# Group order, scratch rows, attention and W3's tails in a fused attention and MLP kernel

## The chip, the cores and the metric

One core of a Trainium2 chip runs the whole kernel. The metric is the device time of one execution in microseconds.

## The reference

With x normalised per row (xn), the output is x + A(xn) + B(xn), for 2048 tokens of 576 channels, all in float32.

```python
def _A_ref(x, wqkv, wo):          # 32 heads of 18, window of 8 keys, every second token
    q, k, v = ...                 # x @ wqkv, split by heads
    idx = pos[:, None] - off[None, :]            # off = 0, 2, ... 14; masked below 0
    logits = einsum("bhsd,bhswd->bhsw", q, kg) * scale
    o = einsum("bhsw,bhswd->bhsd", softmax(logits), vg)
    return o @ wo
def _B_ref(x, w1, w2, w3, w4):
    h = gelu(layernorm(x) @ w1)
    hs = concat(shift(h quarters by +1, -1, +2, -2)) @ w2
    x1 = x + hs
    return x1 + gelu(layernorm(x1) @ w3) @ w4    # w3: 576 x 4608, w4: 4608 x 576
```

## The kernel before

**Numbers in two parts.** Each float32 operand is split into a rounded high part and a low part (the difference), both float32r; a product is three matmuls (high by high, high by low, low by high). Splits are a cast or copy on ScalarE and a subtraction on VectorE.

**Stages.** Normalisation and the product with Wqkv; W1, the shift and W2; then the second MLP (W3, GELU, W4), the largest part; last the product with Wo. Attention itself (products and reductions on VectorE, `attention`) has no stage of its own: it is a generator, and `bg(us, late)` puts as many of its VectorE instructions into the program as a budget allows. Its exponential on ScalarE is put only where `late` is true.

**The second MLP** comes in two forms. First 32 units of a plain product: `up` (a product with 128 columns of W3 for 512 tokens) and `down` (W4, for a tile of 128 tokens). Then 20 groups, 0 to 19 (`q` in the code), that replace eight block products by seven (Strassen's scheme): P1 to P7, each 7 matmuls of 512 columns, and D0 to D7, each a `down` tile of the group before, 12 matmuls of 288 columns. Groups 0 to 9 serve the first half of the tokens, 10 to 19 the second; group 0 has only four tiles. `ORDER` lists the 15 slots of a group, `ORDERS` those of groups 0, 9 and 10. The instruction streams are in program order on each engine; nothing is reordered later.

P1, P6, P7 and P4 accumulate onto one PSUM bank (`ca`) in turn. After P1, P6 and P7 ScalarE copies the sum out (`keep`), and the next of them must wait for the copy. P2's, P5's and P3's results are added in by VectorE (`z_add`). GELU runs on ScalarE twice per block (high part, and full value), `low_part` subtracts on VectorE. The blocks are c11, c12, c21, c22: D0 to D3 read c12 and c22, D4 to D7 c11 and c21. A `down` tile is emptied from one of two PSUM buffers: token tiles in `YD` by ScalarE into a staging row and from there by an accumulating DMA of GpSimd to memory (`yd`), the others by VectorE, added into `Y`.

**Preparing the next group.** `load_pair` (SyncE) reads W3's columns into one staging tile `w3st`; `split_a` makes `w3a` (for P1, P2, P4) from it; `combine`, four VectorE instructions, overwrites the staging with sums; `split_s` makes `w3s` (P5, P6, P7, P3). Both call `split_ws`: steps 0 and 1 are ScalarE's high parts of the main rows and of the 32-row tail (copied on 96 partitions), step 2 VectorE's low parts of both; the tail's low part lies on partitions 32 to 63. `plan` hangs these steps to slots with `at(slot, f, ...)`. `load_w4` and `split_w4` do the same for W4. `split_op` splits the seven operands of the products (B11 ... T4); it writes a high part into a scratch row `r` of `Y` that VectorE then reads, always the same row, `RT`.

In group 15 attention's rest is emitted, its memory is given back, and its result is fetched from memory (`load_o`) and transposed (`o_turn`) for the last stage.

Of the kernel before, what the change touches and what calls it, by code (L numbers as in the profile page):

```python
# [8 lines left out]
F32 = mybir.dt.float32  # L9
# [48 lines left out]
def fused_block(ctx, tc, x, wqkv, wo, w1, w2, w3, w4, out):  # L58
# [717 lines left out]
    EV = ["nt"]  # L776
    RT = temp(2)
    evc = [0]

# [101 lines left out]
    def split_op(sb, k):  # L881
        spent[0] += 1.9
        xt = area[sb][k]
        raw = xt.bitcast(F32)
        sg = -1.0 if k in ("B21", "T1", "T4") else 1.0
        r = RT.bitcast(F32R)
        act.activation(xt[:, 3:5, :], raw[:, 1:3, :], AF.Identity, scale=sg)
        act.activation(r[64:96], raw[64:96, 0, :], AF.Identity, scale=sg)
# [30 lines left out]
    def split_ws(dst, src, steps):  # L919
        if 0 in steps:  # L920
            act.copy(dst[:, 3:5], src[:, 1:3])
        if 1 in steps:
            act.copy(dst[0:96, 0], src[0:96, 0])
        if 2 in steps:
            spent[0] += 1.7
            dve.tensor_tensor(dst[:, 1:3], src[:, 1:3], dst[:, 3:5].bitcast(F32), op=ALU.subtract)
            dve.tensor_tensor(dst[32:64, 0], src[32:64, 0], dst[32:64, 0].bitcast(F32),
                              op=ALU.subtract)

# [18 lines left out]
    LATE = {(0, 0): (12, 13), (0, 1): (14, 15)}  # L948
    RATE = [9.4, 2.0]
    prev = []  # L950
# [5 lines left out]
    for u, (c, b) in enumerate(units):  # L956
        if u == 2:
# [109 lines left out]
    def z_add(dst, ps, z):  # L1067
        spent[0] += 0.69
        dve.tensor_tensor(by_token(dst), in_order(ps), by_token(z), op=ALU.add)  # L1069

    otile, xo = {}, {}
    Wo = None
# [32 lines left out]

    ORDER = "P1 P2 P6 D0 P5 D1 P7 D2 P4 D3 P3 D4 D5 D6 D7"
    ORDERS = {0: "P1 P2 D0 P6 P5 P7 D1 D2 P3 P4 D3",
# [3 lines left out]
    for q in range(NQ):  # L1111
        sb = q // NWP
        p = NPL + pair(q)
        z = q - NQ
        if q:
            h21 = gelu_ps("c21", ca, Z4)
            hid[q - 1, "c21"] = h21
            g = q - 1
            s0 = 8 * (g // NWP)
            w1, w0 = W4[2 * (NPL + pair(g))], W4[2 * (NPL + pair(g)) + 1]  # L1120
            prev = [(s0 + 4 + j, [(hid[g, "c12"], w0), (hid[g, "c22"], w1)]) for j in range(4)]
            prev += [(s0 + j, [(hid[g, "c11"], w0), (h21, w1)]) for j in range(4)]
        if z == -5:
            while not state["done"]:
                bg(1e9)
            apc.__exit__(None, None, None)
            opc = tc.tile_pool(name="op", bufs=1, reuse_waits="tile")
            opool = opc.__enter__()
            evc_pool = tc.tile_pool(name="evp", bufs=1, reuse_waits="tile")
            evp = evc_pool.__enter__()  # L1130
            EV[0] = None
            STS = [place(k).bitcast(F32).rearrange("p a (b c) -> p (a b) c", c=128)
                   for k in range(2)]
            for t in range(3):
                load_o(t)
        if z == -1:
# [30 lines left out]
        if q == 0:  # L1167
            at("P2", split_op, 0, "B22")
            at("P5", split_a, n, (0, 1))
            at("P7", gelu22)  # L1170
            at("P7", split_a, n, (2,))
            at("D1", split_op, 0, "T4")
            at("D2", combine, n)
            at("D2", low22)
            at("D2", split_w4, p)
            at("P3", split_s, n, (0, 1))
            at("P4", split_s, n, (2,))
            at("P4", gelu12)
            at("D3", low12)
            at("D3", load_pair, q + 2)  # L1180
        elif q == NWP - 1:
            at("P1", load_w4, p)
            for it, k in zip(("P1", "P2", "P6", "P5", "P7", "P4", "P3"),
# [11 lines left out]
            at("D7", split_op, 1, "T4")  # L1195
        elif q == NWP:
            at("D1", split_op, 1, "T3")
            at("P2", split_a, n, (0, 1))
# [10 lines left out]
        elif z < -1:  # L1209
            at("P1", load_w4, p)  # L1210
            at("D0", split_a, n, (0, 1))
            at("P5", split_a, n, (2,))
            at("D1", combine, n)
            at("D2", split_w4, p, 0)
            at("P4", split_w4, p, 1)
            at("D3", gelu22)
            at("P3", low22)
            at("P3", split_s, n, (0, 1))
            at("D4", gelu12)
            at("D5", split_s, n, (2,))  # L1220
            at("D6", low12)
            if z < -2:
                at("D6", load_pair, q + 2 + (q == NWP - 2))
        else:
            at("D2", split_w4, p)
            at("D3", gelu22)
            at("D4", low22)
            at("D4", gelu12)
            at("D5", low12)
# [14 lines left out]
        if z == -1:  # L1244
            at("P2", lambda: read_xo(0, xp_tile(2)))
            at("P5", lambda: read_xo(1, ring_block(("o", 1))))
        for it in ORDERS.get(q, ORDER).split():
            if it == "P1":
                ca = product("A11", "B11", q % 2 * 3)
                keep(Z1, ca)  # L1250
                if q:
                    low_part(h21, Z4)
            elif it == "P2":
# [18 lines left out]
            else:  # L1272
                down(*prev[int(it[1])], None)
# [5 lines left out]
    h21 = gelu_ps("c21", ca, Z4)  # L1279
    g = NQ - 1  # L1280
    w1, w0 = W4[2 * (NPL + pair(g))], W4[2 * (NPL + pair(g)) + 1]
    prev = [(12 + j, [(hid[g, "c12"], w0), (hid[g, "c22"], w1)]) for j in range(4)]
    prev += [(8 + j, [(hid[g, "c11"], w0), (h21, w1)]) for j in range(4)]

# [4 lines left out]
    for j in range(8):  # L1289
        down(*prev[j], None)  # L1290
        if j == 0:
# [75 lines left out]
```

## Time and profile before

| | |
|---|---|
| median of three runs | 1296.58 us (1296.18 to 1297.66) |
| profiled execution | 1298.58 us, span 1296.8 us |
| TensorE busy | 1268.3 us, 98% of the span |
| VectorE / ScalarE / GpSimd busy | 971.4 / 596.3 / 214.4 us |
| granted TensorE clock, mean | 0.995 |
| first product of group 0 | 725.32 us into the span |

In the profile PE is TensorE's matmuls, PEld its weight loads, DVE VectorE, ACT ScalarE, POOL GpSimd, SP SyncE; a q behind the engine marks its queue of DMA issues. A window's row gives its length and each engine's busy time in it (instructions in brackets), the granted clock, the share of time that the DMA engines are busy and GB/s. A row of the timeline gives start, length, engine, line, operation, result <- operands, count, and in square brackets the idle time before it and what ended that. Since a product keeps TensorE busy also at a lower clock, lost time is read from a window's length against that of one without a wait.

### The profile page before, as it was taken

The numbers are of one execution on the slowest core, as the hardware profiler recorded it, in microseconds if no ns is written. First come the engines' busy times: TensorE is split into PE (matmuls) and PEld (weight loads), VectorE is DVE, ScalarE is ACT, GpSimd is POOL, SyncE is SP. The second block draws the span as 40 slices with busy tenths as digits, with TensorE's granted clock in tenths as the row PEclk, the third lists the DMA queues.
The fourth block names the chain that finished last, engine by engine and source line by source line (L and its number), as shares of the span: only waits on it lengthen the run. The fifth ranks groups of instructions, "written<-read, shape, count | busy, mean of one in ns | idle before, by whom it ended". The sixth has DMA issues, their size and how long they took to land.

```text
span 1296.8 us, 19623 instructions
## 1 busy us (share of the span) xinstructions
PE 1268.3 (98%) x7538; PEld 1164.3 (90%) x7538; DVE 971.4 (75%) x1299; ACT 596.3 (46%) x952; POOL 214.4 (17%) x318
## 2 busy tenths in 40 slices
PE   8999999999999999999999989999999999899999
PEld 7999998899898998989998878898988998799998
DVE  6456534778469999899989878889888887576542
ACT  3322126526534434344345655655577555455530
POOL 2011100021221212221211111121111121112100
PEclk9999999999999999999999989999999999999999
DMA  7646874246886878989789746568595757899982
GB/s 204 159 115 139 171 172 143 72 133 178 213 249 148 174 166 206 221 155 222 136 183 208 168 107 162 110 114 195 98 247 111 162 101 148 185 215 197 264 257 83
DMA packets 199550, 216.98 MB, mean 167 GB/s; under 512 B 78544, under 2 KB 136528, under 8 KB 199328
## 3 DMA queue, kind: packets, MB, share of 16 engines
q1 hardware_dynamic: 168912, 151.57, 40.5%
q0 software_dynamic: 30544, 64.16, 31.0%
q8 instruction: 59, 0.97, 0.3%
q14 instruction: 35, 0.29, 0.1%
HBM read 119.73 MB, written 107.28 MB: 175 GB/s over the span
## 4 chain that ended last, share of the span: by engine, by line
PE 61%; issue 19%; DVE 7%; DMA 6%; POOL 3%; ACT 3%; SPq 1%; POOLq 0%; DVEq 0%; ACTq 0%
PE ps L828 18%; PE ps L213 16%; PE p L809 9%; PE cc L1059 9%; PE ps L463 4%; POOL yd L833 3%; PE ps L310 3%; DMA yd<-Y 2%; DVE L L735 1%; DMA xt<-td1T 1%; DVE po L732 1%; DVE c L803 1%; PE ps L478 1%; ACT Y L832 1%; DVE Y L837 1%
## 5 line engine op out<-in xcount | busy, mean ns | idle before, releaser
L828 PEld LDWEIGHTS ps<-w,c 128*128 128x128 f32 x3456 | 475.4, 189 | 28.0 <-DVE Y L837 7.8
L828 PE MATMUL ps<-w,c 128*128 128x288 f32 x3456 | 485.7, 296 | 13.7 <-ACT Y L832 5.3
L833 POOL DMA_DIRECT2D yd<-Y x157 | 136.7, 875 | 582.7 <-ACT Y L832 534.0
L832 ACT COPY Y<-ps 128x576 f32<-128x576 f32 x157 | 100.2, 639 | 191.6 <-PE ps L828 136.4
L213 PE MATMUL ps<-WQ,xt 128*128 128x432 f32 x672 | 134.8, 360 | 0.0
L213 PEld LDWEIGHTS ps<-WQ,xt 128*128 128x128 f32 x672 | 125.6, 188 | 5.7
L803 DVE TENSOR_TENSOR c<-Y,c 128x512 fp32r<-128x512 f32 x144 | 98.4, 685 | 38.6 <-ACT Y L792 37.5
L1059 PE MATMUL cc<-xt,w3s 128*128 128x512 f32 x420 | 108.4, 398 | 6.4 <-ACT Y L1065 4.5
L837 DVE TENSOR_TENSOR Y<-ps,Y 128x576 f32<-128x576 f32 x108 | 81.3, 753 | 25.0 <-PE ps L828 24.8
L1059 PEld LDWEIGHTS cc<-xt,w3s 128*128 128x128 f32 x420 | 77.7, 190 | 22.4 <-ACT Y L1065 5.4
L732 DVE TENSOR_TENSOR po<-q,k 128x2304 f32<-128x2304 f32 (+1 forms) x40 | 82.9, 2074 | 16.0 <-issue 10.9
L791 ACT ACTIVATE c<-p 128x512 fp32r<-128x512 f32 x64 | 38.3, 599 | 114.3 <-PE p L809 114.2
L708 DVE TENSOR_TENSOR po<-v,L 128x1152 f32<-128x1152 f32 x64 | 86.2, 1354 | 0.9
L735 DVE TENSOR_REDUCE L<-po 128x128 f32<-128x2304 f32 (+1 forms) x40 | 82.7, 2068 | 0.2
L712 DVE TENSOR_TENSOR po<-po 128x1152 f32<-128x1152 f32 x56 | 75.7, 1353 | 0.6
L120 POOL TENSOR_TENSOR rs<-rs,mhalf 128x1 f32<-128x1 f32 x48 | 30.9, 645 | 258.7 <-DVE rs L119 148.4
L1069 DVE TENSOR_TENSOR Y<-cc,Y 128x512 f32<-128x512 f32 x60 | 41.3, 689 | 39.5 <-PE cc L1059 27.9
L320 ACT COPY stg<-ps 128x864 f32<-128x864 f32 x24 | 21.2, 882 | 102.7 <-PE ps L213 55.8
L1059 PE MATMUL cc<-x1n,w3a 128*128 128x512 f32 (+1 forms) x280 | 67.9, 393 | 0.0
L1065 ACT COPY Y<-cc 128x512 f32<-128x512 f32 x60 | 35.2, 586 | 67.2 <-PE cc L1059 64.5
L1059 PEld LDWEIGHTS cc<-x1n,w3a 128*128 128x128 f32 (+1 forms) x280 | 51.6, 188 | 10.3
L213 PE MATMUL ps<-W,h 128*128 128x288 f32 x384 | 53.5, 295 | 0.0
(186 smaller groups left out, 1888.2 us busy)
## 6 DMA issues: line engine op xcount, KB each, us to landing
yd<-Y POOLq DMA_DIRECT2D x159, 288.0 KB, 5.6
Y<-in_B_w_dram SPq DMA_DIRECT2D x27, 576.0 KB, 7.1
w3st<-in_B_w_dram SPq DMA_DIRECT2D x52, 256.0 KB, 5.6
qkvd<-stg SPq DMA_DIRECT2D x24, 432.0 KB, 3.5
yd<-ev POOLq DMA_DIRECT2D x23, 288.0 KB, 6.4
xd<-st SPq DMA_DIRECT2D x16, 320.0 KB, 6.0
xd<-big SPq DMA_DIRECT2D x16, 320.0 KB, 7.6
w3st<-in_B_w_dram SPq DMA_DIRECT2D x76, 64.0 KB, 5.7
```

Of the source, the lines that this page charges most:

```text
L213: pe.matmul(ps[:, h, :n], xs(a), ws(b, h), start=i == 0, stop=i == len(PAIRS) - 1)
L708: dve.tensor_tensor(dst, vv, Lf[:, :, w:w + 1].to_broadcast([128, TPP * GH, HD]), op=ALU.mult)
L712: dve.tensor_tensor(o, o, dst, op=ALU.add)
L732: dve.tensor_tensor(dst, qf[:, None, :].to_broadcast([128, n, TPP * GC]), win, op=ALU.mult)
L735: dve.tensor_reduce(Lw[:, w:w + n, :], dst.rearrange("p w (x d) -> p w x d", d=HD), axis=AX.X, op=ALU.add)
L803: dve.tensor_tensor(h[:, 1, :], g, h[:, 0, :].bitcast(F32), op=ALU.subtract)
L809: pe.matmul(ps, W3[f][:, w, :], x1n[b][:, a, :], start=n == 0, stop=n == len(PAIRS) - 1)
L828: pe.matmul(ps[:, k, :HF], h[:, col], w[:, p, k * HF:(k + 1) * HF], start=n == 0, stop=n == len(seq) - 1)
L832: act.copy(e.rearrange("p (h c) -> p h c", h=2), ps[:, :, :HF])
L833: pool.dma_start(yd[t], e, accum_op=ALU.add)
L837: dve.tensor_tensor(yv, ps[:, :, :HF], yv, op=ALU.add)
L1059: pe.matmul(ps, WX[w][:k, v, SLOT[w], :], area[sb][xk][:k, a, :], start=onto is None and i == 0, stop=last and i == len(HALVES) - 1, skip_ ...
```

## The change

- The order of slots in the groups: D0 stands one slot earlier, between P2 and P6, and so on. The plan's steps move with it. The two GELUs of c21 come behind the first copy (`keep`) of the next group's P1 instead of ahead of it.
- `split_op` takes its scratch rows in turn from a list: three rows in the last two units, one in group 0, two in group 9, one in group 10.
- The budget of attention per slot is 1.6 instead of 1.5, and 0 instead of 2 in the last two units; the exponential may come at P6 alone, and not in group 9. Attention must be done by P4 of group 14 instead of the start of group 15, and the fetch of its result starts there.
- The low parts of W3's tail rows: ScalarE's instruction for the tail now multiplies by a vector `TS` that is -1 on partitions 32 to 63, and a DMA of GpSimd within SBUF adds the staging's rows to these. The two VectorE instructions of a group on 32 partitions go.

```diff
+    TS = KV[0:96, 2:3]
...
+    pool.memset(TS, 1.0)
+    pool.memset(KV[32:64, 2:3], -1.0)
...
+    rtemps = [2]
...
-        r = RT.bitcast(F32R)
+        rtemps.append(rtemps.pop(0))
+        r = temp(rtemps[-1]).bitcast(F32R)
...
         if 1 in steps:
-            act.copy(dst[0:96, 0], src[0:96, 0])
+            act.activation(dst[0:96, 0], src[0:96, 0], AF.Identity, scale=TS)
+            pool.dma_start(dst[32:64, 0].bitcast(F32), src[32:64, 0], accum_op=ALU.add)
         if 2 in steps:
-            spent[0] += 1.7
+            spent[0] += 1.1
             dve.tensor_tensor(dst[:, 1:3], src[:, 1:3], dst[:, 3:5].bitcast(F32), op=ALU.subtract)
-            dve.tensor_tensor(dst[32:64, 0], src[32:64, 0], dst[32:64, 0].bitcast(F32),
-                              op=ALU.subtract)
...
-    RATE = [9.4, 2.0]
+    RATE = [9.4, 0.0]
...
+        if z == -2:
+            rtemps[:] = [2, 13, 15]
...
-    ORDER = "P1 P2 P6 D0 P5 D1 P7 D2 P4 D3 P3 D4 D5 D6 D7"
+    ORDER = "P1 P2 D0 P6 D1 P5 D2 P7 D3 P4 D4 P3 D5 D6 D7"
...
         elif z < -1:
             at("P1", load_w4, p)
-            at("D0", split_a, n, (0, 1))
-            at("P5", split_a, n, (2,))
-            at("D1", combine, n)
-            at("D2", split_w4, p, 0)
+            at("D1", split_a, n, (0, 1))
+            at("D2", split_a, n, (2,))
+            at("P7", combine, n)
+            at("D3", split_w4, p, 0)
+            at("P4", gelu22)
             at("P4", split_w4, p, 1)
-            at("D3", gelu22)
-            at("P3", low22)
+            at("D4", low22)
             at("P3", split_s, n, (0, 1))
-            at("D4", gelu12)
+            at("D5", gelu12)
             at("D5", split_s, n, (2,))
             at("D6", low12)
...
-            for i, (it, nx) in enumerate((("D1", "P7"), ("D2", "P4"), ("D5", "D6"), ("D6", "D7"))):
+            for i, (it, nx) in enumerate((("P6", "D1"), ("P7", "D3"), ("P3", "D5"), ("D6", "D7"))):
                 t = 4 * (z + 5) + i
                 at(it, o_turn, t)
...
                 keep(Z1, ca)
                 if q:
+                    h21 = hid[q - 1, "c21"] = gelu_ps("c21", cp, Z4)
                     low_part(h21, Z4)
...
-            if z < -5:
-                bg(1.5 - spent[0], it in ("P6", "D1", "P4", "D6"))
+            if z < -6 or z == -6 and EV[0]:
+                bg(1.6 - spent[0], it == "P6" and q != NWP - 1)
                 spent[0] = 0.0
+                if (z, it) == (-6, "P4"):
+                    while not state["done"]:
+                        bg(1e9)
...
+                    for t in range(3):
+                        load_o(t)
```

In group 0, which has four tiles, the steps move too: the split of T4 from D1 to P5, `split_a` of the next weights from P5 and P7 to P7 and D1, `combine` from D2 to P3, `split_w4` from D2 to D3.

The first place is TensorE's stream at the start of group 5, before the change. `cc` are the PSUM banks of the products (the first row is P1, the second P2), `ps` those of the tiles.

```order
L1059 MATMUL cc_7737<-x1n_6399,w3a 128x512 x7
L1059 MATMUL cc_7750<-x1n_6399,w3a 128x512 x7
L1059 MATMUL cc_7737<-xt,w3s 128x512 x7
L828 MATMUL ps_7768<-w_7525,c_7674 128x288 x6
L828 MATMUL ps_7768<-w_7525,c_7644 128x288 x6
L1059 MATMUL cc_7786<-xt,w3s 128x512 x7
```

The same place on TensorE after the change.

```order
L1065 MATMUL cc_7743<-x1n_6401,w3a 128x512 x7
L1065 MATMUL cc_7759<-x1n_6401,w3a 128x512 x7
L832 MATMUL ps_7768<-w_7532,c_7699 128x288 x6
L832 MATMUL ps_7768<-w_7532,c_7652 128x288 x6
L1065 MATMUL cc_7743<-xt,w3s 128x512 x7
L832 MATMUL ps_7797<-w_7532,c_7699 128x288 x6
L832 MATMUL ps_7797<-w_7532,c_7652 128x288 x6
L1065 MATMUL cc_7817<-xt,w3s 128x512 x7
```

D0 (two rows of `ps`) now stands between P2 and P6, and D1 between P6 and P5.

The second place is VectorE in group 5 before the change, from the sum of P2 (L1069) to that of P7. L712 and L708 are attention's, L837 evicts a tile, L926 and L927 make the low parts of `w3a`, L916 is the combine.

```order
L1069 TENSOR_TENSOR Y<-cc_7750,Y 128x512 [waits PE_49,Activation_49]
L712 TENSOR_TENSOR po<-po 128x1152 [waits DVE_49]
L837 TENSOR_TENSOR Y<-ps_7768,Y 128x576 [waits PE_49]
L708 TENSOR_TENSOR po<-v,L 128x1152 [waits DVE_49]
L926 TENSOR_TENSOR w3a<-w3st,w3a 128x768 [waits DMAHW1_49,DMAHW0_49,Activation_49]
L927 TENSOR_TENSOR w3a<-w3st,w3a 32x384 [waits DMAHW3_49,Activation_49]
L916 TENSOR_TENSOR w3st<-w3st 128x3x128 [waits DMAHW4_49,DMAHW5_49,DMAHW2_49,DVE_49]
L916 TENSOR_TENSOR w3st<-w3st 128x3x128 [waits DVE_49] x3
L1069 TENSOR_TENSOR Y<-cc_7786,Y 128x512 [waits Activation_49]
```

VectorE after the change, from the sum of P2 (L1075) on: L735 and L738 are attention's products and reductions, L841 evicts a tile, L932 makes the low part of `w3a`, L807 is c11's low part, L921 the combine.

```order
L1075 TENSOR_TENSOR Y<-cc_7759,Y 128x512 [waits PE_49]
L841 TENSOR_TENSOR Y<-ps_7768,Y 128x576 [waits PE_49]
L735 TENSOR_TENSOR po<-q,k 128x1152 [waits DMAHW0_49,DVE_49]
L738 TENSOR_REDUCE L<-po 128x64 [waits DVE_49]
L735 TENSOR_TENSOR po<-q,k 128x1152 [waits DVE_49]
L738 TENSOR_REDUCE L<-po 128x64 [waits DVE_49]
L841 TENSOR_TENSOR Y<-ps_7829,Y 128x576 [waits PE_49]
L932 TENSOR_TENSOR w3a<-w3st,w3a 128x768 [waits DMAHW1_49,DMAHW0_49,Activation_49]
L1075 TENSOR_TENSOR Y<-cc_7817,Y 128x512 [waits Activation_49]
L807 TENSOR_TENSOR c_7825<-Y,c_7825 128x512
L921 TENSOR_TENSOR w3st<-w3st 128x3x128 [waits DMAHW3_49,DMAHW2_49,DMAHW4_49,DMASW5_49,DMAHW5_49,DMASW2_49,DVE_49]
```

Behind these come three more L921, the low part of W4 and D4's eviction. The row on 32 partitions (L927) is gone. The combine has moved behind the sum of P7, and it now waits for queues of GpSimd's DMAs (DMASW) too.

The third place is GpSimd in a group after the change: L837 are the accumulations of tiles to memory, L929 the new ones within SBUF.

```order
L837 DMA yd_89<-Y 128x576 [waits DMASW3_49,Activation_49]
L929 DMA w3a<-w3st 32x384 [waits DMAHW4_49,Activation_49]
L837 DMA yd_90<-Y 128x576 [waits DMASW5_49,DMASW4_49,Activation_49]
L929 DMA w3s<-w3st 32x512 [waits DVE_49,DMASW6_49,PE_49,Activation_49]
L837 DMA yd_86<-Y 128x576 [waits DMASW7_49,Activation_49]
```

Two DMAs a group are new here, each behind ScalarE's cast of the tail.

More of the change, by code (lines that the diff above doesn't have):

```diff
@@ L1069, in z_add, with downs, plain_downs @@
         dve.tensor_tensor(by_token(dst), in_order(ps), by_token(z), op=ALU.add)
+    def downs(g):
+        s0 = 8 * (g // NWP)
+        w1, w0 = W4[2 * (NPL + pair(g))], W4[2 * (NPL + pair(g)) + 1]
+        for j in range(8):
+            if j < 4:
+                yield lambda j=j: down(s0 + 4 + j, [(hid[g, "c12"], w0), (hid[g, "c22"], w1)], None)
+            else:
+                yield lambda j=j: down(s0 + j - 4, [(hid[g, "c11"], w0), (hid[g, "c21"], w1)], None)
+    def plain_downs():
+        for t, parts in prev:
+            yield lambda t=t, parts=parts: down(t, parts, None)
     otile, xo = {}, {}
@@ L1114, in fused_block @@
         z = q - NQ
[L1115 to L1135, printed above, removed]
+        cp = ca if q else None
+        if q == 0:
+            rtemps[:] = [2]
         if z == -1:
@@ L1196, in fused_block @@
         elif q == NWP:
+            rtemps[:] = [2]
             at("D1", split_op, 1, "T3")
@@ L1227, in fused_block @@
             at("D4", low22)
-            at("D4", gelu12)
-            at("D5", low12)
+            at("D5", gelu12)
+            at("D6", low12)
             for k, it in enumerate(("D5", "D6", "D7")):
@@ L1246, in fused_block @@
             at("P5", lambda: read_xo(1, ring_block(("o", 1))))
+        tiles = list(downs(q - 1) if q else plain_downs())
         for it in ORDERS.get(q, ORDER).split():
@@ L1272, in fused_block @@
             else:
-                down(*prev[int(it[1])], None)
+                tiles[int(it[1])]()
             for f in plan.get(it, ()):
                 f()
-            if z < -5:
-                bg(1.5 - spent[0], it in ("P6", "D1", "P4", "D6"))
+            if z < -6 or z == -6 and EV[0]:
+                bg(1.6 - spent[0], it == "P6" and q != NWP - 1)
                 spent[0] = 0.0
[L1279 to L1283, printed above, removed]
+                if (z, it) == (-6, "P4"):
+                    while not state["done"]:
+                        bg(1e9)
+                    apc.__exit__(None, None, None)
+                    opc = tc.tile_pool(name="op", bufs=1, reuse_waits="tile")
+                    opool = opc.__enter__()
+                    STS = [place(k).bitcast(F32).rearrange("p a (b c) -> p (a b) c", c=128)
+                           for k in range(2)]
+                    evc_pool = tc.tile_pool(name="evp", bufs=1, reuse_waits="tile")
+                    evp = evc_pool.__enter__()
+                    EV[0] = None
+                    for t in range(3):
+                        load_o(t)
+    h21 = hid[NQ - 1, "c21"] = gelu_ps("c21", ca, Z4)
+    tiles = list(downs(NQ - 1))
     def load_y(ts):
@@ L1289, in fused_block @@
     for j in range(8):
-        down(*prev[j], None)
+        tiles[j]()
         if j == 0:
```

17 lines of the change are left out of this document (9 added, 8 removed).

## The prediction

> **What bounds the kernel now.** I read the page first, then busy times in windows cut where a group's first product starts, then the timeline around each wait of TensorE, then instructions by form and the DMA issues.
>
> ```profile
> PE 1268.3 (98%) x7538; PEld 1164.3 (90%) x7538; DVE 971.4 (75%) x1299; ACT 596.3 (46%) x952; POOL 214.4 (17%) x318
> ```
>
> ```profile
> core 0: us, PE busy (x) PEld busy (x) DVE busy (x) ACT busy (x) POOL busy (x), PEclk, DMA share, GB/s
> 700.56:725.32 24.76, 21.39 (x126) 19.68 (x125) 21.66 (x26) 16.12 (x25) 3.17 (x4) 0.93 0.66 166
> 743.49:773.76 30.27, 26.98 (x147) 24.16 (x146) 21.76 (x29) 15.81 (x25) 3.80 (x5) 0.89 0.37 79
> 773.76:945.61 171.85, 169.12 (x1017) 153.52 (x1016) 151.37 (x172) 95.47 (x150) 30.26 (x36) 1.00 0.65 137
> 945.61:997.10 51.49, 49.20 (x292) 44.07 (x291) 43.91 (x55) 40.51 (x61) 8.48 (x11) 1.00 0.76 182
> 997.10:1093.69 96.59, 96.45 (x582) 87.78 (x581) 86.08 (x103) 52.68 (x84) 17.42 (x21) 1.00 0.66 137
> 1093.69:1123.71 30.02, 26.19 (x147) 23.28 (x146) 16.58 (x28) 13.19 (x21) 4.31 (x6) 0.94 0.79 170
> 1123.71:1219.90 96.19, 96.19 (x583) 87.75 (x581) 59.47 (x95) 51.44 (x82) 17.33 (x21) 1.00 0.95 225
> ```
>
> The rows are the units' end, group 1, groups 2 to 8, 9 and 10, 11 to 14, 15, and 16 to 19. TensorE bounds the kernel: in the last row it is busy for the whole 96.19 us, so a group without a stall takes 96.19/4 = 24.05 us, a slot (one of its 15 products and tiles) 1.60. Only the excess over this can be won: 30.27 - 24.05 = 6.2 in group 1, 171.85 - 7 x 24.05 = 3.5 in groups 2 to 8, 3.4 in 9 and 10, 0.4 in 11 to 14, 6.0 in 15; and 24.76 - 21.39 = 3.4 idle at the units' end. The granted clock tells of a second loss behind the waits:
>
> ```profile
> 708.26:712.00 3.74, 3.74 (x15) 0.54 0.96 192
> 750.17:753.60 3.43, 3.43 (x9) 0.50 1.02 241
> 753.60:757.00 3.40, 3.40 (x16) 0.63 0.75 238
> ```
>
> These rows (TensorE alone) follow two waits. At the units' end the lower clock costs 3.74 x 0.46 = 1.7 us more; in group 1 it costs 1.7 + 1.3, which the 6.2 already holds.
>
> **Part by part: the places where TensorE waits.**
>
> ```profile
> 706.40 0.63 ACT L888 ACTIVATE Y<-x1n 32x512 fp32r<-32x512 f32 x1 [3.34 <-DVE x1n L591]
> ...
> 708.26 3.23 PE L828 MATMUL ps<-w,c 128*128 128x288 f32 x12 [2.56 <-ACT Y L832]
> ...
> 723.62 1.86 PE L828 MATMUL ps<-w,c 128*128 128x288 f32 x12 [0.81 <-DVE Y L837]
> ```
>
> *Units' end.* L888 writes the scratch row and waits 3.34 us until VectorE has read it for the operand before. The eviction behind it comes late and TensorE waits 2.56. With scratch rows in turn L888 doesn't wait, and the last two units have no attention, so that VectorE has three attention instructions less there. I take 3.4 + 1.7 = 5.1 less a rest of 0.5: **-4.6**. Next in line is VectorE's eviction, whose 0.81 is in this.
>
> ```profile
> 742.01 2.33 DVE L916 TENSOR_TENSOR w3st<-w3st 128x384 f32<-128x384 f32 x4
> ...
> 744.42 1.06 ACT L921 CAST w3s<-w3st 128x1024 fp32r<-128x1024 f32 x1 [2.73 <-DVE w3st L916]
> ...
> 750.17 3.35 PE L1059 MATMUL cc<-xt,w3s 128*128 128x512 f32 x7 [3.29 <-ACT Y L1065]
> ```
>
> *Group 1.* VectorE, still behind from group 0, combines late; ScalarE's cast waits 2.73 for it; the copy of P1's sum comes late, and P6 waits 3.29. Now D0 stands ahead of P6 (1.6 us more) and the copy ahead of the two GELUs of c21 (1.2 us). Group 0's queue by these durations: combine done 18.4 us after its start, cast w3s 20.1, a tile's copy 20.7, cast W4 21.9, copy of P1's sum 22.5, and P6 would start about 23: no wait. But D0, now a slot earlier, wants W4 at 20.8 to 21.4: it waits some 0.8 us for the cast and about 1 for its low part. With half a clock drop I leave 3.0 of 6.2: **-3.2**.
>
> ```profile
> 951.26 1.28 ACT L750 ACT_TABLE_LOAD   x1
> ...
> 956.33 1.89 PE L1059 MATMUL cc<-xt,w3a 128*128 128x512 f32 x7 [0.90 <-ACT Y L1065]
> ```
>
> *Groups 9 and 10.* The exponential with its table loads fell between P6 and P4 in group 9, where the order is tight; it may no longer come there, and a second scratch row frees ScalarE in group 9's five operand splits. I leave 1.2 of 3.4: **-2.2**.
>
> ```profile
> 1110.24 0.71 DVE L159 STREAM_TRANSPOSE big<-Y 128x512 f32<-128x512 f32 x1 [5.35 <-DMA Y<-od]
> ...
> 1111.78 1.87 PE L1059 MATMUL cc<-xt,w3s 128*128 128x512 f32 x7 [1.85 <-DVE Y L1069]
> ...
> 1115.27 1.15 ACT L563 CAST w<-Y 128x1152 fp32r<-128x1152 f32 x1 [9.53 <-DMA Y<-in_B_w_dram]
> ...
> 1117.02 2.52 PE L828 MATMUL ps<-w,c 128*128 128x288 f32 x12 [1.78 <-ACT ev L832]
> ```
>
> *Group 15.* The last attention rows are stored and read back at once; VectorE waits 5.35 us for the first, and W4's load, behind these on SyncE's queue, holds ScalarE 9.53. Now the rows are fetched at P4 of group 14 and first transposed at P6 of group 15, 9 slots or 14 us later, and the order shows attention's last instruction in group 11 already (twelve groups, not fourteen; that costs nothing). I leave 0.3 of 6.0: **-5.7**.
>
> *Groups 2 to 8 and 11 to 14.* VectorE's load decides:
>
> ```profile
> L708 DVE TENSOR_TENSOR po<-v,L 128x1152 f32<-128x1152 f32 x64 | 86.2, 1354 | 0.9
> L837 DVE TENSOR_TENSOR Y<-ps,Y 128x576 f32<-128x576 f32 x108 | 81.3, 753 | 25.0 <-PE ps L828 24.8
> L732 DVE TENSOR_TENSOR po<-q,k 128x2304 f32<-128x2304 f32 x24 | 61.3, 2554 | 4.9 <-DMA od<-po 4.7
> L916 DVE TENSOR_TENSOR w3st<-w3st 128x384 f32<-128x384 f32 x76 | 42.4, 558 | 2.6
> L1069 DVE TENSOR_TENSOR Y<-cc,Y 128x512 f32<-128x512 f32 x60 | 41.3, 689 | 39.5 <-PE cc L1059 27.9 <-ACT Y L1065 11.1
> L926 DVE TENSOR_TENSOR w3a<-w3st,w3a 128x768 fp32r<-128x768 f32 x19 | 18.1, 951 | 0.0
> L927 DVE TENSOR_TENSOR w3s<-w3st,w3s 32x512 fp32r<-32x512 f32 x19 | 12.9, 682 | 0.6
> L927 DVE TENSOR_TENSOR w3a<-w3st,w3a 32x384 fp32r<-32x384 f32 x19 | 10.4, 548 | 0.7 <-ACT w3a L923 0.2
> ```
>
> The tails' instructions go: 0.68 + 0.55 = 1.23 us a group. Counting the order's attention instructions by these durations, groups 1 to 8 held 63.6 us and now hold 90.0. VectorE was busy 21.8 + 151.4 = 173.1 us there, 21.6 a group; now 21.6 + 26.4/8 - 1.2 = 23.7 of 24.05. That nearly fills it, so the place of each wait matters. The tightest is D6, whose PSUM buffer must have been emptied of D4: D4 ends 17.6 us into a group, D6 starts at 20.8, two slots apart where before it was one. In group 5 VectorE runs from the sum of P2 to D4's eviction 0.69 x 3 + 0.75 x 3 + 1.35 x 5 + 0.95 + 4 x 0.56 = 14.3 us, so may start at 6.5, where P2's data is there at 3.4; in group 6, the worst, 16.5, so 4.3. By the same adding-up it comes to that run 5.9 us into group 6, and D6 waits a microsecond or so. A gain of a slot against a fuller queue: I keep the 3.5 + 0.4 as they are, **0**, with -3.9 and the rival's price below as ends.
>
> **The new DMAs.** Neither trace row shows an accumulation within SBUF. Nearest:
>
> ```profile
> yd<-Y POOLq DMA_DIRECT2D x159, 288.0 KB, 5.6
> ...
> td1T<-xn POOLq DMA_DIRECT2D x2, 576.0 KB, 9.1
> ...
> v<-u SPq DMA_DIRECT2D x32, 32.0 KB, 1.9
> ```
>
> A plain SBUF copy of 32 KB lands in 1.9 us, an accumulation of 288 KB in 5.6, the slowest group in 9.1. The tails are 48 and 64 KB in 32 rows; by size they lie near the first, and I take 3. Who waits: the combine on VectorE (it overwrites what the w3a tail reads), with all of VectorE's queue behind it; SyncE, whose next W3 load overwrites the staging, with W4's load behind; TensorE last. In group 5 ScalarE has cast the w3a tail 10.2 us in, GpSimd issues at 10.6, the combine comes at 16.4 at the latest: covered up to **5.8** us. The w3s tail issues at 21.5 and lands at 24.5; the load waits for it:
>
> ```profile
> 897.52 3.39 PE L1059 MATMUL cc<-x1n,w3a 128*128 128x512 f32 x14
> ...
> 904.04 0.51 ACT L923 CAST w3a<-w3st 96x384 fp32r<-96x384 f32 x1 [0.16 <-DMA w3st<-in_B_w_dram]
> ...
> 919.63 0.38 SPq L905 DMA_DIRECT2D w3st<-in_B_w_dram  x1
> ```
>
> Before, it starts 919.63 - 897.52 (group 7's P1) = 22.1 in and its last piece lands 6.5 into the next group; after the change 24.5 and 8.9. The w3a casts moved a slot back, their tail to 9.7: covered by 0.8. So the DMAs cost **0**.
>
> **Sum.** -4.6 - 3.2 - 2.2 - 5.7 = -15.7. The profiled execution took 1298.58 us around its span of 1296.8, 0.9 over the slowest of the three timed runs. The terms are differences within that span; taken from the median, 1296.58, they give 1280.9: **1281 us**. 0.2% (2.6 us) is about what a measurement here can tell from no change.
>
> *A page's rule.* The Trainium skill (TensorE: Matmul & The Clock Gate, Part 1) halves the clock after an idle window of about 3.4 us. The row behind the 2.56 us wait shows 0.54, so here a shorter wait is enough. By the rule group 1's new waits would cost no clock, the sum would be about 1280.
>
> **The rivals.**
>
> *VectorE becomes the bound in groups 1 to 8.* For: 23.7 of 24.05. Its waits for P2 and P7's sums were 39.5/60 = 0.66 us each, three a group: 23.7 + 2.0 = 25.7, or 1.6 x 8 = 13 us, which gives 1294. Against: two thirds of those waits are for TensorE, and go when VectorE is behind. With half of it 1287 to 1291, still faster; at its full price with one more term missed, no change.
>
> *The tails land late (slower).* Each microsecond over 5.8 delays the combine and a full VectorE in groups 1 to 8 and 11, 9 us in all. At 5.8 + 15.7/9 = 7.5 us the gain is gone; at 9.1, the slowest row, 3.3 x 9 = 30 and 1311 us. For: the w3a tail is issued behind a 288 KB accumulation on the same queue, and must land under DMA engines 65% busy. Against: its size and the 1.9.
>
> The Trainium skill (SBUF — State Buffer, Who interferes with whom) adds that VectorE's two-port modes block GpSimd's building of descriptors. An issue on GpSimd takes 0.86 us in the timeline next to a VectorE that is 88% busy:
>
> ```profile
> 919.64 0.86 POOL L833 DMA_DIRECT2D yd<-Y  x1 [3.93 <-ACT Y L832]
> ```
>
> [...]
>
> **How the numbers follow.** Forecast 0.59 (1275 to 1287), VectorE bound but faster 0.17 (1287 to 1294), no change within 0.2% 0.07, late tails 0.17. Faster 0.76, same 0.07, slower 0.17. The range 1275 to 1296 leaves out the late tails and a few in a hundred below.
>
> **What would show it.** Right: no scratch wait at L888, group 15 near 24.3 us, group 1 near 27, granted clock 1.00 at the units' end, tails landing under 5.8 us. Wrong: VectorE's combine waiting for a GpSimd DMA, groups 2 to 8 over 24.6 each, or waits of D6 for VectorE in most of them.

## The result, and the profile after

The changed kernel takes 1305.05 us (median of 16 runs, 1300.29 to 1312.13), the kernel before, on the same chips, 1296.26 (16 runs). The ratio is 1.0065, 95% interval 1.0045 to 1.0084: it became slower, and 1305 lies outside the range 1275 to 1296.

The profiled execution took 1301.97 us around a span of 1300.2; before it was 1298.58 around 1296.8. So the traces hold 3.4 us of the 8.8 between the medians. The rest was seen in no trace: the profiled run of after is one of its faster ones, that of before one of its slower ones.

The page after (busy time, then the slices that hold the loss, each 1300.2/40 = 32.5 us):

```profile
PE 1266.0 (97%) x7538; PEld 1161.7 (89%) x7538; DVE 944.6 (73%) x1261; ACT 598.2 (46%) x952; POOL 245.2 (19%) x358
...
PE   8999999999999999999999999999959999999999
...
PEclk9999999999999999999999999999979999999999
```

One slice stands out in both rows: number 30 from the left, 943 to 975 us. The windows of after, cut as before where a group's first product starts: the last four units, group 1, groups 2 to 8, 9 with 10, 11 to 14, 15, 16 to 18, and 19:

```profile
655.80:718.99 63.19, 63.01 (x378) 57.27 (x376) 58.74 (x61) 36.57 (x56) 13.38 (x17) 1.00 0.84 197
```

```profile
736.65:763.54 26.89, 24.85 (x148) 21.90 (x146) 22.19 (x25) 15.93 (x24) 5.94 (x7) 1.00 0.73 159
763.54:932.47 168.93, 168.93 (x1018) 153.66 (x1017) 160.60 (x177) 99.36 (x153) 41.86 (x50) 1.00 0.71 144
932.47:997.93 65.46, 50.63 (x292) 45.00 (x291) 46.02 (x55) 37.54 (x58) 10.28 (x13) 0.90 0.78 172
997.93:1094.17 96.24, 96.24 (x582) 87.75 (x581) 58.89 (x77) 53.01 (x84) 23.81 (x29) 1.00 0.69 136
1094.17:1118.23 24.06, 24.06 (x147) 21.94 (x146) 14.68 (x24) 13.31 (x21) 5.98 (x8) 1.00 0.79 170
1118.23:1195.08 76.85, 72.97 (x437) 65.89 (x436) 45.18 (x75) 40.28 (x63) 17.69 (x21) 1.00 0.95 212
1195.08:1223.67 28.59, 25.87 (x147) 23.16 (x145) 9.18 (x14) 11.00 (x19) 4.32 (x5) 0.94 0.97 255
```

Against the lengths before (68.22 for the last four units, the others as the prediction shows them, or 24.05 a group) these are -5.0, -3.4, -2.9, **+14.0**, -0.4, -6.0, **+4.7** (76.85 - 3 x 24.05) and **+4.5**. Group 0 is 0.5 shorter, and what lies ahead of and behind these stages is 1.7 us shorter together. The gains are there; three places that the prediction gave nothing, or a gain, cost 23 us.

**Group 9.** TensorE's longest wait of the whole kernel, and VectorE's:

```profile
942.13 1.79 PE L1065 MATMUL cc<-xt,w3a 128*128 128x512 f32 x7
957.45 3.29 PE L1065 MATMUL cc<-xt,w3s 128*128 128x512 f32 x7 [13.54 <-DVE Y L1075]
```

```profile
939.67 0.69 DVE L705 TENSOR_TENSOR L<-L,mx 128x512 f32<-128x512 f32 x1
954.17 2.63 DVE L711 TENSOR_TENSOR po<-v,L 128x1152 f32<-128x1152 f32 x2 [13.80 <-DMA v<-qkvd]
956.71 0.68 DVE L1075 TENSOR_TENSOR Y<-cc,Y 128x512 f32<-128x512 f32 x1
```

P3 waits for the sum that belongs to P7 (L1075). It stands on VectorE's queue behind two multiplications of attention (L711), and the first of these waits 13.80 us for `v`. Why `v` is late stands in the chain of work that ended last (start, length, what):

```profile
929.88 2.50 DMA w3s<-w3st
...
936.26 9.55 DMA x1n<-xn
945.87 0.53 SPq L717
946.40 0.05 issue
946.45 2.22 SPq L692
...
949.27 6.13 DMA xt<-td1T
```

L717 is the store of attention's seventh eighth (`od`), L692 the fetch of `v` for its last. Both are SyncE's, whose queue in group 9 also carries the operands of the second half. VectorE had the store's data ready at 937.85, the end of its last addition. SyncE was then still issuing loads of operands that stand ahead, until 943.25, and the queue's waits (in total, times, longest) say what held the store from there until 945.87:

```profile
936.50 1.35 DVE L715 TENSOR_TENSOR po<-po 128x1152 f32<-128x1152 f32 x1
...
941.51 1.74 SPq L883 DMA_DIRECT2D x1n<-xn  x3
```

```profile
SPq L717 <- DMA x1n<-xn: 2.6, 1, 2.6
```

It waits for the landing of an operand's load that stood ahead. The second piece of `v`, issued behind the store at 948.73, lands 5.4 us later, at 954.09, and only a few VectorE instructions are left between fetch and use, since the last eighth has no q by k part to fill them. Of VectorE's 13.80 us some 8.0 are the queue's (937.85 to 945.87). The other 5.8, an estimate by subtraction, are the issue and the flight of the fetch itself, which nothing covers. In the kernel before, the same store and the same multiplication came in group 12, and the latter's row has no wait (SyncE first, then VectorE):

```profile
1027.04 0.53 SPq L714 DMA_DIRECT2D od<-po  x1
```

```profile
1036.78 2.62 DVE L708 TENSOR_TENSOR po<-v,L 128x1152 f32<-128x1152 f32 x2
```

**Groups 16 to 18.** The same two queues in each; here group 16, GpSimd, VectorE and TensorE:

```profile
1129.74 0.79 POOL L929 DMA_DIRECT2D w3a<-w3st  x1 [1.34 <-ACT w3a L928]
```

```profile
1135.61 2.34 DVE L921 TENSOR_TENSOR w3st<-w3st 128x384 f32<-128x384 f32 x4 [2.40 <-issue]
```

```profile
1140.73 3.44 PE L832 MATMUL ps<-w,c 128*128 128x288 f32 x24 [1.45 <-DVE Y L841]
```

The tail's accumulating DMA is issued at 1129.74 and lands 5.70 us later, at 1135.43; combine, which overwrites what it reads, starts at 1135.61. Behind it on VectorE stand a transpose of attention's result and W4's low part, then the eviction of D4, and D6, which needs D4's PSUM buffer, waits (the third of these rows). Landing times (count, KB, median us), first groups 2 to 8, then 16 to 18:

```profile
w3s<-w3st POOLq DMA_DIRECT2D x7, 64.0 KB, 2.5
w3a<-w3st POOLq DMA_DIRECT2D x7, 48.0 KB, 3.3
```

```profile
Y<-od SPq DMA_DIRECT2D x41, 72.0 KB, 3.9
...
w3s<-w3st POOLq DMA_DIRECT2D x3, 64.0 KB, 3.4
w3a<-w3st POOLq DMA_DIRECT2D x3, 48.0 KB, 5.9
```

The medians hide two late tails of `w3a` in groups 2 to 8: 5.0 us in group 3 and 6.1 in group 5. There combine waited too, 1.64 us in group 5, but TensorE didn't. So a late tail alone is not yet a loss. In group 16 the DMA was issued 11.5 us into the group instead of 10.4 in group 5, and the transpose stands behind combine.

**Group 19.** ScalarE's queue around P4:

```profile
1210.73 1.15 ACT L566 CAST w<-Y 128x1152 fp32r<-128x1152 f32 x1 [5.58 <-DMA Y<-in_B_w_dram]
1211.79 0.58 ACT L1071 COPY Y<-cc 128x512 f32<-128x512 f32 x1
```

```profile
1212.42 2.79 PE L1065 MATMUL cc<-xt,w3a 128*128 128x512 f32 x7 [2.72 <-ACT Y L1071]
```

The plan of group 19 still hangs the split of W4 to D2, but in the new order D2 stands ahead of P7, so P7's copy now waits behind a cast that waits for W4's load.

### The profile page after: what moved, and what is told of

It reads as the page before. It is cut to its first block, busy times and chain, and to the rows that moved or that the text cites. A ratio compares the mean times of both kernels' runs of the same rounds, so it can differ in the third digit from the quotient of the medians.

```text
span 1300.2 us, 19681 instructions
## 1 busy us (share of the span) xinstructions
PE 1266.0 (97%) x7538; PEld 1161.7 (89%) x7538; DVE 944.6 (73%) x1261; ACT 598.2 (46%) x952; POOL 245.2 (19%) x358
## 4 chain that ended last, share of the span: by engine, by line
PE 78%; DMA 10%; DVE 4%; issue 4%; ACT 2%; SPq 1%; POOL 0%; DVEq 0%; POOLq 0%; ACTq 0%
PE ps L832 27%; PE ps L214 16%; PE cc L1065 13%; PE p L813 13%; PE ps L466 4%; PE ps L313 3%; DMA w3st<-in_B_w_dram 2%; DMA x1n<-xn 1%; DMA yd<-Y 1%; DMA xn<-st 1%; DMA xt<-xn 1%; DMA w3a<-w3st 1%; DMA xt<-xd 1%; DMA wr<-in_A_wo_dram 1%; PE ps L481 1%
## 5 line engine op out<-in xcount | busy, mean ns | idle before, releaser
L837 POOL DMA_DIRECT2D yd<-Y x154 | 137.0, 894 | 464.7 <-ACT Y L836 388.4
L807 DVE TENSOR_TENSOR c<-Y,c 128x512 fp32r<-128x512 f32 x144 | 98.4, 685 | 58.8 <-ACT Y L796 42.3
L841 DVE TENSOR_TENSOR Y<-ps,Y 128x576 f32<-128x576 f32 x108 | 81.2, 751 | 49.2 <-PE ps L832 49.0
L711 DVE TENSOR_TENSOR po<-v,L 128x1152 f32<-128x1152 f32 x64 | 86.1, 1353 | 14.7 <-DMA v<-qkvd 13.8
L735 DVE TENSOR_TENSOR po<-q,k 128x2304 f32<-128x2304 f32 (+1 forms) x40 | 82.9, 2073 | 13.9 <-issue 11.6
L738 DVE TENSOR_REDUCE L<-po 128x128 f32<-128x2304 f32 (+1 forms) x40 | 82.8, 2069 | 0.4
L715 DVE TENSOR_TENSOR po<-po 128x1152 f32<-128x1152 f32 x56 | 75.8, 1353 | 0.8
L813 PE MATMUL p<-xt,w3s 128*128 128x512 f32 x224 | 52.4, 390 | 0.0
```

The source lines that it names most:

```text
L711: dve.tensor_tensor(dst, vv, Lf[:, :, w:w + 1].to_broadcast([128, TPP * GH, HD]), op=ALU.mult)
L715: dve.tensor_tensor(o, o, dst, op=ALU.add)
L735: dve.tensor_tensor(dst, qf[:, None, :].to_broadcast([128, n, TPP * GC]), win, op=ALU.mult)
L738: dve.tensor_reduce(Lw[:, w:w + n, :], dst.rearrange("p w (x d) -> p w x d", d=HD), axis=AX.X, op=ALU.add)
L807: dve.tensor_tensor(h[:, 1, :], g, h[:, 0, :].bitcast(F32), op=ALU.subtract)
L813: pe.matmul(ps, W3[f][:, w, :], x1n[b][:, a, :], start=n == 0, stop=n == len(PAIRS) - 1)
```

## The experiments

My theory: three losses of their own, each a wait in an engine's or a queue's order. Rivals: VectorE's work piles up in group 9 whatever the queue holds; `v` is late because the DMA engines are full; the tails' DMAs slow everything; the new order itself.

**The last eighth later.** The work of attention's last eighth begins 16 us of other work later; the store and the fetch ahead of it stay where they were on SyncE's queue.

```diff
             if g:
+                if g == NG:
+                    yield 16.0
                 yield from av(g - 1)
```

> Attention's last eighth starts 16 us of budget (ten slots) later; all else as in the changed kernel, so its two multiplications no longer stand in group 9 ahead of the sum of P7. Theory (the fetch of v, queued behind the second half's operands, held VectorE 13.8 us and so TensorE 13.5): the wait goes, group 9 takes 25 to 27 us, the span falls by 14 to 16 us, the time to 1284 to 1290. Rival (the loss lies in the order or in late tails, and would come out elsewhere): 1297 or more, with stalls in groups 9 to 13.

1295.42 us (12 runs), ratio to the kernel before 0.9979 (0.9964 to 0.9995). The wait for `v` is gone and group 9 takes 29.4 us instead of 40.1, but not the 25 to 27 expected. Now it is the other users of the queue that come late: the split of T2, whose load stands behind the store and the fetch, and D7, whose PSUM buffer is emptied behind that split. D7 starts at 960.94, after a wait of 4.49 us.

```profile
957.91 1.06 ACT L894 ACTIVATE xt<-xt 128x1024 fp32r<-128x1024 f32 x1 [3.75 <-DMA xt<-td1T]
```

So the time expected was missed by 5 us or more: with VectorE out of the way, the loads behind the store and the fetch are the next to come late.

**Tails by VectorE.** The two VectorE instructions come back, and the accumulating DMAs go.

```diff
-            act.activation(dst[0:96, 0], src[0:96, 0], AF.Identity, scale=TS)
-            pool.dma_start(dst[32:64, 0].bitcast(F32), src[32:64, 0], accum_op=ALU.add)
+            act.copy(dst[0:96, 0], src[0:96, 0])
...
+            dve.tensor_tensor(dst[32:64, 0], src[32:64, 0], dst[32:64, 0].bitcast(F32),
+                              op=ALU.subtract)
```

> The changed kernel with the tails' low parts on VectorE again, attention's budget kept so that its order does not move. Theory: the wait for v in group 9 stays (12 to 15 us); VectorE, 1.2 us a group fuller, falls behind in groups 1 to 8, where the groups take up to 1 us more each; the combine no longer waits in groups 16 to 18, 4 us less there: 1302 to 1312. Rival (the accumulating DMAs are the cause of the loss): 1294 or less.

1303.57 us (12 runs), ratio 1.0036 (1.0021 to 1.0051), within the 1302 to 1312 expected. So the tails' DMAs are not the cause of the whole loss. Groups 16 to 18 have no stall (first row; the second is groups 2 to 8):

```profile
1124.21:1196.39 72.18, 72.18 (x438) 65.82 (x436) 49.48 (x82) 39.79 (x63) 12.98 (x16) 1.00 0.96 217
766.22:937.82 171.60, 169.53 (x1018) 153.69 (x1016) 168.00 (x189) 98.99 (x153) 30.06 (x35) 1.00 0.68 138
```

The order of slots is that of after, and the DMA engines are as busy (0.96), so the 4.7 us there are the tails' DMAs. But groups 2 to 8 take 171.6 us instead of 168.9, so there the DMAs bring the 2.7 (in the other traces that keep the DMAs these groups take 168.4 to 169.6 us). Group 9 stays at 40.0: its loss has nothing to do with the tails.

**W4's split behind P7's copy**, in group 19 alone.

```diff
-            at("D2", split_w4, p)
+            at("P7", split_w4, p)
```

> The changed kernel with the split of W4 in group 19 hung to P7, behind the copy of P7's sum on ScalarE, instead of D2 ahead of it. Theory: the copy no longer stands behind a cast that waits for W4's load; group 19 takes 25 us instead of 28.6, the time falls by 3 to 4 us. Rival (W4's load is itself too late for the group): the wait moves to the tiles and nothing is won.

1303.77 us (7 runs), ratio 1.0045 (1.0027 to 1.0062): 1.3 us less than the changed kernel, where 3 to 4 were expected. In the trace group 19 takes 24.17 us instead of 28.59, and TensorE has no wait left in it, so the third loss is shown in its stage:

```profile
1198.87:1223.04 24.17, 24.17 (x146) 21.97 (x145) 8.06 (x11) 11.02 (x19) 3.46 (x4) 1.00 0.99 242
```

The same trace loses most of this ahead of group 19: groups 9 and 10 take 67.4 us instead of 65.5, and group 18 27.7 instead of 25.8, by the two losses that this edit leaves in. Whether that holds for the other runs as well, no trace shows.

**The fetch of v on GpSimd's queue**, for the last eighth alone.

```diff
-                    vs[g] = load("v", 2, g, True)
+                    vs[g] = load("v", 2, g, True, pool if g == NG - 1 else sp)
```

> The changed kernel with the last fetch of v on GpSimd's queue instead of SyncE's; VectorE's order is the same to the row. Theory (its place in SyncE's queue is what made v late): it is issued about 7 us sooner, VectorE waits 4 to 8 us instead of 13.8, the time falls by 5 to 9 us. Rival (it lands late because the DMA engines are full with the operands): it lands at the same time, no change.

1310.51 us (6 runs), ratio 1.0089 (1.0059 to 1.0118): no better, where 5 to 9 us less were expected. Group 9 begins at 938.94 in this trace, not at 932.47. From there `v` lands 13.8 us in (at 952.8) instead of 21.6, and VectorE waits longer, for the other of the two:

```profile
961.82 2.63 DVE L711 TENSOR_TENSOR po<-v,L 128x1152 f32<-128x1152 f32 x2 [14.97 <-DMA od<-po]
```

```profile
949.18 5.49 SPq L883 DMA_DIRECT2D x1n<-xn  x3
956.24 0.52 SPq L717 DMA_DIRECT2D od<-po  x1
```

The first multiplication overwrites what the store reads, and the store still stands behind the operands' loads. These now fly beside the fetch: the load that the store waits for takes 13.1 us to land instead of 9.6, the two pieces of `v` 9.4 and 10.6 instead of 6.3 and 5.4. So what I had named, the fetch, was half of it, and the load on the DMA engines has a part in the wait. Of the 9.0 us by which this trace is longer than that of the changed kernel, 6.1 lie ahead of group 0, which begins at 725.11 instead of 718.99; the edit changes nothing there.

**No attention in group 9**, and 8 us of other work ahead of the last eighth.

```diff
+                if g == NG:
+                    yield 8.0
...
-            if z < -6 or z == -6 and EV[0]:
+            if q == NWP - 1:
+                spent[0] = 0.0
+            elif z < -6 or z == -6 and EV[0]:
```

> The changed kernel, but no attention is emitted in group 9, and attention's last eighth begins with 8 us of other work: the store of od and the fetch of v then stand on SyncE's queue behind the operand loads of the second half, in group 10, and no multiplication follows the fetch at once. Theory (the 14 us of group 9 are VectorE's wait for a store and a fetch that share SyncE's queue with the operand loads, in either order): groups 9 and 10 together take 50 to 52 us instead of 65.5, no wait for v or for an operand above 2 us, and the kernel takes 1287 to 1291 us, 14 us less than the changed kernel. Rival (group 9 is long because VectorE's work of two groups piles up there, whatever the queue holds): groups 9 and 10 stay above 58 us and the time stays above 1296 us.

1291.38 us (12 runs), ratio 0.995 (0.9928 to 0.9972). Groups 9 and 10:

```profile
933.84:960.27 26.43, 24.84 (x148) 21.96 (x146) 15.66 (x19) 16.84 (x27) 4.13 (x5) 1.00 1.01 248
960.27:986.70 26.43, 24.64 (x147) 21.96 (x146) 19.85 (x26) 20.57 (x32) 6.17 (x8) 1.00 0.77 177
```

52.9 us instead of 65.5: 12.6 of the 14.0 are back, with a mean clock of 1.00 instead of 0.90, just outside the 50 to 52 expected, as is the time with 1287 to 1291. This run also takes attention's work out of group 9 (VectorE is busy 35.5 us in the two groups instead of 46.0), so it can't refute the pile-up rival by itself; the trace of the changed kernel does, where VectorE sat idle for 13.80 us. That the place of the store and the fetch on SyncE's queue decides is shown by this run, the last eighth later and the fetch on GpSimd's queue together; each alone left a way out.

**All three mended.** The kernel of the last run, with two things more: where `dvt` is set, in groups 13 to 18, `split_ws` has VectorE's instruction instead of the DMA, and in group 19 the split of W4 is hung to P7.

```diff
+        dvt[0] = q >= 13
...
-            at("D2", split_w4, p)
+            at("P7", split_w4, p)
```

> The kernel of the run e5_no_att_9, with the tails of groups 13 to 18 by VectorE as before the change, and in group 19 the split of W4 hung to P7, behind P7's own copy. Theory (the three losses are separate and add up): groups 15 to 19 take 24.1 us each, 9 to 10 us less than in e5_no_att_9, groups 1 to 8 as there; the kernel takes 1277 to 1281 us, about 16 us less than the kernel before. Rival (what is won in groups 15 to 19 is given back later, in the last eight tiles or at the output projection, or groups 13 and 14 run into VectorE): above 1284 us.

1283.56 us (6 runs), ratio 0.9876 (0.9853 to 0.9899); on a chip where the kernel before took 1298.66 that is 15 us less, where 16 were expected; the time itself lies above the 1277 to 1281 named. Groups 16 to 18 take 72.18 us and group 19 24.08. Nothing of note comes back later (behind group 19 the trace has 77.2 us, that of the changed kernel 76.5), so the losses add up.

**Scratch rows alone**, on the kernel before, in the last two units.

```diff
+    rtemps = [2]
...
-        r = RT.bitcast(F32R)
+        rtemps.append(rtemps.pop(0))
+        r = temp(rtemps[-1]).bitcast(F32R)
...
+        if z == -2:
+            rtemps[:] = [2, 13, 15]
...
+        if q == 0:
+            rtemps[:] = [2]
```

> The kernel before, with one part of the change alone: the scratch rows of the operands' splits are taken in turn in the last two units; attention runs there as before. Theory of the prediction (what the units' end gained came from the rows, since each split waited for the signed copy of the split ahead): the last four units and the way to group 0 take 63 to 64 us instead of 68.2, and the kernel takes 4 to 5 us less than the kernel before. Rival (it came from attention, which the change keeps out of the last two units): the stage stays at 67 to 68 us and the time within 1 us.

1293.97 us (10 runs), ratio 0.9961 (0.9944 to 0.9978). The last four units:

```profile
656.50:720.21 63.71, 63.00 (x378) 57.28 (x376) 60.69 (x64) 36.39 (x56) 12.56 (x15) 1.00 0.83 195
```

4.5 of the 5.0 us at the units' end are the rows; keeping attention out has at most 0.5.

**Combine a slot later**, on the changed kernel. D3 is the slot right behind P7, so the step moves by one tile.

```diff
-            at("P7", combine, n)
+            at("D3", combine, n)
```

> The changed kernel, with combine hung to D3 instead of P7 in groups 1 to 8 and 11 to 18, one product and one tile later. Theory (groups 16 to 18 are longer because combine waits on VectorE for the DMA of w3a's tail rows, which lands 2.3 to 6.1 us after its issue, with the eviction of a tile queued behind it): groups 16 to 18 take 24.1 to 24.4 us each instead of 25.3 to 25.8, and the kernel takes 4 to 5 us less than the changed kernel, unless the later combine delays the halves of w3s behind it. Rival (the order of products and tiles alone makes these groups long): they stay at 25 us or more.

1305.23 us (12 runs), ratio 1.005 (1.003 to 1.007), no gain: groups 16 to 18 took 25.2, 25.4 and 26.7 us. Combine still waits for the DMA, since this landed later as well:

```profile
w3s<-w3st POOLq DMA_DIRECT2D x3, 64.0 KB, 3.8
w3a<-w3st POOLq DMA_DIRECT2D x3, 48.0 KB, 6.8
```

In group 17 it was issued at 1157.29, landed at 1164.05, and combine began at 1164.13. Combine moved, and the wait for the DMA moved with it; the slot that I gave it was not enough.

**Tails of groups 1 and 10 by VectorE too.** In the run with all three mended, combine still waited 3.2 us in group 1 and 2.8 in group 10. The tail of `w3a` took 6.1 us to land in both, in group 10 with the fetch of `v` in flight.

```diff
-        dvt[0] = q >= 13
+        dvt[0] = q in (1, NWP) or q >= 13
```

> The kernel of the run e6_best, with the tails of groups 1 and 10 by VectorE too: in that run combine waits 3.17 us in group 1 and 2.76 us in group 10, where the w3a tail lands 6.1 us after its issue or shares the DMA engines with the fetch of v. Theory (a tail DMA is free only in groups where no other loads are in flight at its time): group 1 takes 25.5 to 26 us instead of 27.2 and group 10 25.3 to 26 us instead of 27.6, the groups 2 to 9 stay, and the kernel takes 3 to 4 us less than e6_best, 0.985 of the kernel before. Rival (VectorE is short of time in these two groups and the 1.2 us more on it come back as later sums): the two groups stay within 0.5 us and the ratio stays at 0.9876.

1279.13 us (6 runs), ratio 0.986 (0.9829 to 0.989): faster than both kernels. Group 1 takes 25.47 us and group 10 25.33, as expected. Its ratio and that of the run with all three mended have intervals that overlap; that it is the faster of the two rests on the traces (span 1277.0 against 1279.4).

```profile
738.35:763.82 25.47, 24.58 (x147) 21.88 (x146) 24.18 (x28) 15.69 (x24) 4.50 (x6) 1.00 0.73 161
763.82:932.24 168.42, 168.42 (x1018) 153.56 (x1016) 159.94 (x176) 99.13 (x153) 41.79 (x50) 1.00 0.73 144
932.24:983.34 51.10, 49.20 (x293) 44.01 (x291) 36.90 (x46) 37.44 (x58) 8.66 (x11) 1.00 0.90 218
```

## Why the prediction was wrong

- **Units' end, -4.6:** right, -5.0, and by the rows, as it said (4.5 by them alone).
- **Group 1, -3.2:** right in size, -3.4, at a clock of 1.00. Of the 2.8 us that stayed, TensorE's timeline shows a wait of 0.86 inside D0 for W4's low part, where some 1.8 had been worked out, and one of 1.16 ahead of D6, behind combine: the tail's DMA again, which the prediction had at nothing. With VectorE's tails it goes.
- **Group 15, -5.7:** right, -6.0; no stall is left.
- **Groups 2 to 8, 0:** too careful. They became 2.9 us shorter, 24.13 a group. VectorE was busy 160.6 of 168.9 us, 95%, and yet TensorE was busy all the time, so the rival of VectorE as the bound did not come about. With the two tail instructions back (run with tails by VectorE) 2.7 us return, so this gain is the tails', not the order's.
- **Groups 9 and 10, -2.2: the step that failed.** It came out at +14.0. The prediction removed the exponential and freed ScalarE's splits, and did not follow what the faster attention moves. In the group 15 part it says that attention ends in group 11 already, and that this "costs nothing". That is the wrong sentence: with attention's last store in group 11 instead of 15, the store of the seventh eighth and the fetch of `v` for the last move from group 12 into group 9, on SyncE's queue, among the operand loads of the second half. There VectorE waits 13.80 us for them, and TensorE 13.54 behind VectorE. The order of SyncE was not read beside that of VectorE. With +14.0 for -2.2 the sum of -15.7 would have been +0.5.
- **The new DMAs, 0: a second step that failed,** in its sizes. Landing was put at 3 us by size, from a row of 32 KB and one of 288. The tails of `w3a` took 2.6 to 6.1 us in groups 2 to 8 and 5.7 to 6.0 in groups 16 to 18, so size did not decide. The same view of the kernel before had a row of 64 KB (count, KB, median us) that says as much:

```profile
w3st<-in_B_w_dram SPq DMA_DIRECT2D x76, 64.0 KB, 5.7
```

The cover of 5.8 us was too large as well. In group 5, for which it was worked out, combine could have begun 4.6 us after the issue (852.57 less its wait of 1.64, from 846.37), in group 16 3.5 (1135.61 less 2.40, from 1129.74). The price was 4.7 us in groups 16 to 18 and part of group 1. The rival of late tails had the mechanism, and looked for it in groups 1 to 8 and 11 with a full VectorE instead. The prediction's signs of being wrong, combine waiting for a GpSimd DMA and D6 for VectorE, came true, though only in some of the groups.
- **Group 19:** no term at all. The plan's line for it was unchanged; but D2 had moved from behind P7 to ahead of it. It cost 4.5 us.
- **The clock.** Behind the 13.54 us wait it was low again, 0.53 for the next 3.29 us:

```profile
957.45:960.74 3.29, 3.29 (x9) 2.65 (x10) 3.23 (x5) 0.00 (x0) 0.00 (x0) 0.53 1.03 247
```

That is in the +14.0. The Trainium skill's rule on the idle window (TensorE: Matmul & The Clock Gate, Part 1), about 3.4 us, would have this drop too; here it tells nothing that the 2.56 us wait did not.

What made tails late can be read from single ones: the stretches from issue to landing of the `w3a` tails of groups 5, 7, 12 and 16 in the changed kernel.

```profile
846.37:852.48 6.11, 6.11 (x38) 5.50 (x37) 4.46 (x6) 3.31 (x6) 1.58 (x2) 1.00 1.16 288
895.60:898.86 3.26, 3.26 (x22) 2.96 (x21) 3.23 (x4) 2.73 (x4) 0.77 (x1) 1.00 0.74 106
1032.41:1035.64 3.23, 3.23 (x21) 2.92 (x20) 1.62 (x2) 1.43 (x3) 0.77 (x1) 1.00 0.77 107
1129.74:1135.43 5.69, 5.69 (x35) 5.12 (x34) 2.85 (x4) 3.94 (x7) 1.68 (x2) 1.00 1.06 272
```

In groups 7 and 12 VectorE is busy for 99% and 50% of the stretch, and the tail takes the same 3.2 to 3.3 us. In groups 5 and 16 the DMA engines are busy throughout (shares of 1.16 and 1.06 instead of 0.74 and 0.77; packets count where they start, so that a share can pass 1), and it takes 5.7 to 6.1. So these rows speak for the load on the DMA engines and against VectorE; no run changed that load alone. The 288 KB accumulation ahead on GpSimd's queue, which the prediction named, is the other candidate: in groups 5, 7 and 12 the tail lands 0.2 to 0.6 us behind it, but in group 16 2.4 us, so it is not all. The Trainium skill's section on VectorE's hold over GpSimd's descriptors (SBUF — State Buffer, Who interferes with whom) speaks of two-port modes, and gives `tensor_tensor` none. In group 7's stretch VectorE runs nothing else (L711, L715, L841, L932), and the tail takes the 3.26 us of a quiet one, so this trace agrees; the rule gave no reason to look for late tails where VectorE is full of `tensor_tensor`.

What stays open: the 5 us between the medians that lie outside the two traces. The part of the program ahead of group 0 varies by more than that where the program is the same: group 0 begins at 717.55 us in the run with the last eighth later, at 718.99 in the changed kernel, at 725.11 with the fetch on GpSimd's queue. That the 5 us lie there is not shown.

## What to carry to other kernels

A budget that speeds up background work also moves its transfers: for each store and fetch that it issues, read what stands ahead of it on its queue in the new place, what it stands ahead of, and how much work is left between fetch and use. When an order of slots changes, go through every table that refers to the slots, the unchanged lines first, since there a step's meaning has changed without a diff. And an operation that is handed to a DMA has a price that goes with what else is in flight; use it in the stages where the queues are quiet, and the engine in the others.

## What the runs showed of the hardware

An accumulating DMA within SBUF of 48 KB in 32 rows landed 3.2 to 3.3 us after its issue where the DMA engines were busy for 0.74 to 0.77 of its flight, and 5.7 to 6.1 where they were busy throughout (1.06 and 1.16), whether VectorE was busy for 99% or 50% of the stretch in the one case and 73% or 50% in the other. A store on SyncE whose data was ready waited, by the profile, 2.6 us for the landing of a load ahead of it that it had no data in common with, so that the queue's order costs more than its issue times. VectorE at 95% in groups 2 to 8 did not slow TensorE, which was busy the whole time. In the traces of all these runs, the kernel before included, no TensorE wait of up to 1.73 us had a drop of the clock by itself (1.73 in the run with W4's split behind P7's copy: 1.00 for the 3.32 us behind it), and every one of 2.72 us or more had one (2.72 in group 19 of the changed kernel: 0.60 for the next 3.38). Between, both occur: 1.94 us in group 18 of the run with W4's split behind P7's copy with a drop (0.66 for the next 4.70), 2.65 us in group 19 of the run with combine a slot later without one (1.00 for the next 3.32).
